# An attention gate feeding a capacity-limited mixture of experts: last rows transposed on TensorE, all table rows kept on chip, tail weights split on VectorE, z requested three lane steps ahead

## The chip, the cores and the metric

The kernel runs on one core of one Trainium2 chip, in one launch. The metric is the device time of one execution in microseconds. Before the change three timed runs took 1415.2, 1415.2 and 1415.48 us, median 1415.2. One more execution was profiled; its time is 1417.8 us, and its trace spans 1416.1 us from the first to the last instruction.

Engine names are those of the trace: PE is TensorE's matmuls, PEld its weight loads, DVE is VectorE, ACT ScalarE, POOL GpSimd, SP SyncE. SPq and POOLq are the instructions that these two engines issue to the DMA queues.

## The reference

Eight batches of 2496 rows, 256 wide, with 64-wide keys z. Each batch computes squared-ReLU attention with z as queries and keys, multiplies the result by u, and the 19968 rows of all batches go into a mixture of eight experts. A row goes to the expert with the largest logit; an expert that has more than 80 rows keeps the 80 with the largest gate weight. All other rows of the output are zero.

```python
scores = (1.0 / S) * np.matmul(z, z.transpose(0, 2, 1))
attn = np.maximum(scores, 0.0) ** 2
x = (u * np.matmul(attn, v)).reshape(B * S, D)        # B, S, D = 8, 2496, 256

logits = x @ w_gate                                    # 8 experts
expert_idx = np.argmax(logits, axis=1)
gate_w = softmax(logits)[np.arange(N), expert_idx]
for e in range(E):
    tok_idx = np.where(expert_idx == e)[0]
    if len(tok_idx) > capacity:                        # 80
        gw = gate_w[tok_idx]
        tok_idx = tok_idx[np.argpartition(-gw, capacity)[:capacity]]
    h = np.maximum(x[tok_idx] @ w1[e], 0.0)            # 256 x 1024
    out[tok_idx] = gate_w[tok_idx, None] * (h @ w2[e]) # 1024 x 256
```

The gate weights of nearly all rows are equal when rounded, so which rows an expert keeps is decided by position in the order that the reference's partition leaves; the kernel works out those positions from counts of rows per expert. Where this does not hold, a flag sends the kernel into a general path behind the measured one.

## The kernel before

**Numbers.** A large matmul operand is held as a high part (rounded) and a low part (the rest), and a product is three matmuls: high by high, low by high, high by low. ScalarE mostly rounds the high part, VectorE subtracts to get the low one. This split is done for z, v, the attention matrix, the expert weights w1 and w2 and the gathered rows.

**The attention.** A batch has 20 tiles of 128 rows, taken in five chunks of 512 rows (the last has 448). For each chunk the keys are taken in ten pairs of tiles. The matrix is symmetric: a pair is either computed (`scores`, then ReLU, square, split) or read back as the mirrored block of an earlier chunk (`mirrored`), which was transposed on VectorE, written to DRAM (`y`) and read (`blk`). Two chunks run at a time, as two lanes, half a chunk apart. A lane step `t` is one pair of each lane; five steps are half a chunk, 25 steps a batch. The order in which TensorE, ScalarE, VectorE and SyncE take their instructions is the order of the program text (`manual_schedule`); GpSimd is put under it too from the experts on.

**z and v for the next batch.** At the end of each lane step `z_and_v(t)` looks up tables by the step within the batch: `Z_LOAD` requests a 256 KB piece of z into the one buffer `zraw`, `Z_SPLIT` lets VectorE split it into `zs` (or `zm` for piece 0), `Z_COPY` copies it across partitions by DMA. A split stands before the next request, which needs its buffer. SyncE issues all DMAs of the attention in order, each waits for the semaphore of an earlier one, so at most eight are under way.

**A finished chunk** goes through `finished(b, qc, r)`, r being the pair of the next chunk beside which a part is put: x = u times the accumulators (VectorE and ScalarE), its rows transposed by two DMAs (`chunk_store`, L530) and stored to DRAM `xs` (`chunk_store2`), x split into three bf16 parts (`chunk_hi`, `chunk_rest`, `chunk_mid`, `chunk_lo`), gate logits by 24 small matmuls (`chunk_logits`, L554), and per batch the top-1, the gate weights, and the counts of rows per expert and block of 256 rows. `blocks` (L691 to L696) makes for each block a table row of running counts by three matmuls, rounds it on ScalarE and writes it to the DRAM table `wtab`. Near the end one lane is left, and `finished_late` does the same work for the last chunk but one.

**The end of the attention.** The weights of experts 0 and 1 are loaded and split beside the last chunks (`weights_ahead`); the raw weights of expert 2 wait in buffers (`kept`). Four further pieces of weights, 512 KB each, are requested near the last pair. Then x of the last 448 rows is made, its rows go through the DMA transposes, its logits through fp32 matmuls, and the top-1, the counts and the ranks of the 80 slots follow on VectorE. For experts 0 and 1 TensorE makes the table rows (`pe_table`) and picks each slot's row by a one-hot matmul (`pe_block`, `pe_fetch`); for experts 2 to 7 GpSimd reads the rows from `wtab` by six indirect DMAs (`fetches`).

**An expert.** VectorE compares its table row with the slot's rank and gets the token number (`token`), GpSimd gathers the 80 rows (`xg`), VectorE puts their halves together (`whole`), TensorE transposes them (`ffn_x`), two halves of the first product follow (`ffn1`, six matmuls each), ReLU on ScalarE, a transpose and a split (`ffn_h`), the second product (`ffn2`, 24 matmuls), and on ScalarE the scaling by the gathered gate weight; GpSimd scatters the rows to the output (`result`). `target` gathers the gate weights, which the last gate write (`gate_put`, elements of 4 bytes, L642) must have left in DRAM. `split(n)` splits the next n pieces of weights and requests as many new ones. For expert 2 three of the four low halves are left to the experts' part: one on VectorE, two on GpSimd (`half_lo(PL)`).

Of the kernel before, what the change touches and what calls it, by code (L numbers as in the profile page):

```python
# [26 lines left out]
def attn_moe_kernel(ctx, tc, zT, uT, v, wg, w1, w2, out, seq, cap):  # L27
# [504 lines left out]

    def chunk_store2(b, qc):
# [224 lines left out]

    def halves_hi(n):

        for _ in range(n):
            p, raw = kept.pop(0)
            halves.append(split_w(*p, raw, None))
            nc.scalar.copy(out=halves[-1][1], in_=raw)
# [47 lines left out]
    N_PE = 2  # L812
    wq_t, le_g, bo_g = [], [], []

    def scratch():

        t = vpool.tile([P, 2048], F32, tag="vt", name="scratch")
        n = [N_PE * P, 2 * (1 + NBLK), (E - 2) * (1 + NBLK), N_PE * NBLK]
        o = [sum(n[:i]) for i in range(5)]
        w = t[:, :o[1]].bitcast(BF16)  # L820
        wq_t.extend(w[:, e * 2 * P:(e + 1) * 2 * P] for e in range(N_PE))
        le_g.append(t[:, o[1]:o[2]].rearrange("p (e k) -> p e k", e=2))
        le_g.append(t[:, o[2]:o[3]].rearrange("p (e k) -> p e k", e=E - 2))
        bo_g.append(t[:, o[3]:o[4]].rearrange("p (e k) -> p e k", e=N_PE))

    def pe_table(e):

        wp = ps_s.tile([P, CH], F32, tag="s", name=f"wq_{e}")
        ev, od = oh[:, 0, :, e], oh[:, 1, :, e]
        nc.tensor.matmul(wp[:NBLK, :P], ev, upper, start=True, stop=True)  # L830
        nc.tensor.matmul(wp[:NBLK, P:2 * P], ev, ones_b, start=True, stop=False)
        nc.tensor.matmul(wp[:NBLK, P:2 * P], od, upper, start=False, stop=True)
        nc.scalar.copy(out=wq_t[e][:NBLK], in_=wp[:NBLK, :2 * P])
# [9 lines left out]
    WARM = 3  # L843
# [4 lines left out]
    def weights_ahead(qc, r):  # L848
        if not places:
# [6 lines left out]
            places.extend([None] * NW + [vv, a4[0], xt])  # L856
        if (qc, r) in SPLITS:
            p = SPLITS[qc, r]
            split_w(*p, w_raw.pop(p), V)
# [12 lines left out]
    def finished(b, qc, r):  # L872
# [22 lines left out]
        if qc == 0 and b > 0:  # L895
# [3 lines left out]
            elif r == 6:  # L899
                up_to(*part)  # L900
                blocks(ps_m, "m", gp, oh, *part)
# [3 lines left out]
    def finished_late(b, qc, r):  # L905
# [37 lines left out]
    if True:  # L943
# [150 lines left out]
        for i in range(e, len(entries)):  # L1094
# [4 lines left out]
            if i == e + HALF:  # L1099
                logits(n)  # L1100
                prev = at(n + 1)
                chunk_x(*prev)
            if i + 2 < len(entries) and i > e:
# [11 lines left out]
            else:  # L1115
                if i == e + HALF:
                    finished(*at(n), NP)
                if i == e + HALF + 1:
# [3 lines left out]
            if i == len(entries) - 2:  # L1122
# [3 lines left out]
                loads(4)  # L1126
# [16 lines left out]
        for e in range(N_PE):  # L1143
            pe_table(e)
# [170 lines left out]
    def steps_of(own, tl, tw, ps_t, ps_h):  # L1315
# [69 lines left out]
        def many_within():  # L1385
            le = le_g[1][:, :, 1:]
            tt(le, le, tot[:, es], ALU.mult)
            V.tensor_reduce(out=small["exc"][:, es], in_=le, axis=AX.X, op=ALU.add)
            tt(small["rin"][:, es], rank[:, 0, es], small["exc"][:, es], ALU.subtract)
            ts(small["base"][:, es], small["cnt"][:, es], float(2 * P), ALU.mult)  # L1390

        def fetches():

            rest = slice(N_PE, E)
            ix = tl.tile([P, E - N_PE], F32, name="ix")
            V.scalar_tensor_tensor(out=ix, in0=small["cnt"][:, rest], scalar=float(E),
                                   in1=first_w[:, 0, rest], op0=ALU.mult, op1=ALU.subtract)
            idx = tl.tile([P, E - N_PE], I32, name="idx_rest")
            ts(idx, ix, float(E), ALU.add)

            def one(u):
                ns, i = num(u), u - N_PE
# [339 lines left out]
```

## Time and profile before

| | |
|---|---|
| timed runs, median of 3 | 1415.2 us |
| profiled execution | 1417.8 us, span 1416.1 us |
| TensorE busy (matmuls) | 1360.8 us, 96% |
| VectorE, ScalarE, GpSimd busy | 1072.6 (76%), 1024.5 (72%), 47.5 us (3%) |
| DMA moved | 319.12 MB, mean 225 GB/s |
| granted TensorE clock, mean | 0.979 |

The attention takes all but the last 100 us. In it TensorE is busy without a break except at a few waits, and the other engines have time left; in the last 100 us no engine is busy throughout. In the rows below a line of a timeline is: start, time taken, engine, line of the kernel, operation, output and inputs with their shapes, count, and in brackets the idle time of the engine just before with what ended it.

### The profile page before, as it was taken

Reading aid. Unit: us, or ns where it says so; the run is one execution under the profiler, and the core shown is the slowest. Engines: PE = TensorE matmul, PEld = TensorE weight load, DVE = VectorE, ACT = ScalarE, POOL = GpSimd, SP = SyncE. Lnnn points to the kernel's source line nnn. Section 1 sums busy time; section 2 is a strip of 40 time slices with the busy share of each in tenths; the row PEclk is TensorE's granted clock in tenths of the full one; section 3 lists DMA queues with packets and bytes.
Section 4 is the critical chain, followed back from the end, with each engine's and each line's share of the span. In section 5 each row is a group of like instructions: output and inputs, shape, how many; then the busy total and the mean of one; then the engine's idle time right before and its main releaser. Section 6 shows DMA issues by size and latency. Waiting matters only on the chain. (4 is left out here: it accounts for less than half of the span.)

```text
span 1416.1 us, 30052 instructions
## 1 busy us (share of the span) xinstructions
PE 1360.8 (96%) x12033; PEld 1136.1 (80%) x12033; DVE 1072.6 (76%) x1558; ACT 1024.5 (72%) x1321; POOL 47.5 (3%) x52
## 2 busy tenths in 40 slices
PE   8998999999999999999999999999999999999586
PEld 5887887888977888788887888888887888777374
DVE  6776787787877877877877777877778777877675
ACT  6876697677876697677877587777877688775254
POOL 0000000000000000000000000000000000000164
PEclk9999999999999999999999999999999999999689
DMA  5699869997979969998879958998879957899543
GB/s 173 183 267 279 203 187 238 250 270 209 246 190 286 222 164 258 252 275 217 237 190 262 258 155 239 261 267 215 244 207 231 292 162 211 241 291 279 151 139 112
DMA packets 265956, 319.12 MB, mean 225 GB/s; under 512 B 98654, under 2 KB 190834, under 8 KB 255570
## 3 DMA queue, kind: packets, MB, share of 16 engines
q1 hardware_dynamic: 264594, 315.58, 83.2%
q8 instruction: 96, 1.57, 0.5%
q0 software_dynamic: 1216, 1.56, 0.5%
q14 instruction: 50, 0.41, 0.1%
HBM read 153.48 MB, written 126.37 MB: 198 GB/s over the span
## 5 line engine op out<-in xcount | busy, mean ns | idle before, releaser
L441 PE MATMUL acc<-ah,vt 64*128 64x512 f32 (+1 forms) x6004 | 831.2, 389 | 1.1 <-ACT vt L108 0.6
L441 PEld LDWEIGHTS acc<-ah,vt 64*128 64x128 f32 x6004 | 602.3, 186 | 101.5 <-DVE vt L159 1.5
L441 PE MATMUL acc<-al,vt 64*128 64x512 f32 (+1 forms) x3002 | 480.9, 387 | 0.2 <-DVE al L55 0.2
L55 DVE TENSOR_TENSOR al<-a,ah 128x1024 fp32r<-128x1024 f32 (+1 forms) x240 | 291.4, 1214 | 172.1 <-ACT ah L370 133.6
L364 ACT ACTIVATE a<-s 128x512 f32<-128x512 f32 (+1 forms) x480 | 258.7, 591 | 181.6 <-PE s L361 178.5
L441 PEld LDWEIGHTS acc<-al,vt 64*128 64x128 f32 x3002 | 310.6, 185 | 50.3 <-DVE al L55 0.6
L367 ACT ACTIVATE a<-a 128x1024 f32<-128x1024 f32 (+1 forms) x240 | 253.1, 1055 | 7.4
L55 DVE TENSOR_TENSOR al<-blk,ah 128x1024 fp32r<-128x1024 f32 x160 | 193.7, 1211 | 50.1 <-PE acc L441 23.5
L342 ACT CAST ah<-blk 128x1024 fp32r<-128x1024 f32 x160 | 167.3, 1047 | 85.2 <-PE acc L441 77.0
L297 DVE STREAM_TRANSPOSE x<-a 128x512 f32<-128x512 f32 x320 | 207.5, 687 | 0.0
L370 ACT CAST ah<-a 128x1024 fp32r<-128x1024 f32 x160 | 168.0, 1050 | 5.1
L361 PE MATMUL s<-zm,zs 64*128 64x512 f32 x960 | 145.2, 394 | 1.6 <-DVE zs L121 1.2
L361 PEld LDWEIGHTS s<-zm,zs 64*128 64x128 f32 x960 | 95.2, 184 | 21.0 <-ACT a L364 1.8
L361 PE MATMUL s<-zm 64*128 64x512 f32 x480 | 74.7, 405 | 1.9 <-ACT a L364 1.9
L375 DVE CAST ah<-a 128x1024 fp32r<-128x1024 f32 (+1 forms) x80 | 53.8, 673 | 29.7 <-ACT a L367 29.6
L361 PEld LDWEIGHTS s<-zm 64*128 64x128 f32 x480 | 48.2, 187 | 10.7 <-ACT a L364 2.7
L1449 POOL DMA_INDIRECT xg<-xs,tok x8 | 9.2, 1146 | 1340.0 <-DMA wtab<-wb 1333.8
L159 DVE TENSOR_TENSOR vt<-vraw,vt 128x1024 fp32r<-128x1024 f32 (+1 forms) x40 | 46.1, 1153 | 6.6 <-ACT vt L108 6.6
L554 PEld LDWEIGHTS <-xb 128*128 128x128 bf16 x936 | 26.7, 96 | 30.2 <-DVE xb L55 16.5
L554 PE MATMUL pl<-wgs,xb 128*128 128x24 bf16 x936 | 31.3, 174 | 15.8 <-DVE xb L55 15.8
L55 DVE TENSOR_TENSOR xb<-xf,xb 128x1024 bf16<-128x1024 f32 (+1 forms) x38 | 45.2, 1191 | 0.2
L108 ACT CAST vt<-vraw 128x1024 fp32r<-128x1024 f32 (+3 forms) x56 | 44.9, 829 | 0.0
(169 smaller groups left out, 786.8 us busy)
## 6 DMA issues: line engine op xcount, KB each, us to landing
y<-x SPq DMA_DIRECT2D x80, 1024.0 KB, 7.1
blk<-y SPq DMA_DIRECT2D x320, 256.0 KB, 6.6
out<-idle SPq DMA_DIRECT2D x40, 512.0 KB, 3.7
vraw<-v SPq DMA_DIRECT2D x32, 512.0 KB, 7.0
zm<-zs SPq DMA_DIRECT2D x128, 128.0 KB, 7.1
ut<-uT SPq DMA_DIRECT2D x32, 512.0 KB, 7.3
xs<-xq SPq DMA_DIRECT2D x32, 512.0 KB, 7.1
wraw<-w SPq DMA_DIRECT2D x28, 512.0 KB, 6.4
```

The lines of the kernel that those rows point to most:

```text
L55: V.tensor_tensor(out=o, in0=a, in1=b, op=op)
L108: eng.copy(out=o, in_=i)
L159: e1.tensor_tensor(out=vt[:, :nf, 1], in0=raw[:, :nf], in1=vt[:, :nf, 0], op=ALU.subtract)
L297: V.transpose(out=x[:, :, :, t].rearrange("p n k s -> p k n s"), in_=a)
L342: nc.scalar.copy(out=natural(ah), in_=src)
L361: nc.tensor.matmul(s, zk, zm[rows, :, y].rearrange("p h k t -> p k h t"), start=i == 0, stop=i == 2)
L364: nc.scalar.activation(out=a[:, h, :nq], in_=s[:, :nq], func=AF.Relu)
L367: nc.scalar.activation(out=a[:, :, :nq], in_=a[:, :, :nq], func=AF.Square)
L370: nc.scalar.copy(out=st["ah"][:, :, :nq], in_=a[:, :, :nq])
L375: V.tensor_copy(out=ah[:, :, :nq], in_=a[:, :, :nq])
L441: ins = nc.tensor.matmul(acc[c], vt, a[rows, k % 2, :nq], start=p == pairs[0] and group == 0 and i == 0, stop=p == pairs[-1] and group == ...
L554: nc.tensor.matmul(pl[:, t * n:(t + 1) * n], xb[:, i % 3, i // 3, t0:t0 + P], wgs[:, i // 3].rearrange("p s e -> p (s e)"), start=i == 0, ...
```

## The change

1. The last 448 rows are transposed on TensorE in eight blocks, copied by ScalarE as 16-bit halves in the order of the store, and stored by two DMAs (`chunk_rows_last`).
2. TensorE makes the table rows of all eight experts behind the last chunk (`pe_tables`, two experts per bank) and keeps them on chip; the slots of experts 2 to 7 pick their rows by one-hot matmuls (`many_pe`, `many_fetch`). `blocks` is no longer called in the batches and at the end, and the six indirect reads go.
3. The low halves of expert 2's weights and one of expert 1's are split on VectorE, four in a row beside expert 1. The order of the experts' part is written out anew up to expert 1; the last gate write comes before the first expert, the splits of later weights start beside expert 1 with two pieces, and go on with four per expert.
4. z's pieces are requested three lane steps before their split. The logits of the third chunk from the end come one entry later, and so do some parts of the chunk behind it.

```diff
+    def chunk_rows_last(b, qc):
...
+        for t0 in range(0, QT, 2):
+            xp = ps_a.tile([P, CH], F32, tag="acc", name=f"xp_{b}_{qc}_{t0}")
+            for t in (t0, t0 + 1):
+                q0 = min(t * P, nq - P)
+                for c in range(DC):
+                    nc.tensor.transpose(out=xp[:, (t - t0) * D + c * P:(t - t0) * D + (c + 1) * P],
+                                        in_=xf[:, c, q0:q0 + P], identity=ident)
+            nc.scalar.copy(out=xq[:, t0:t0 + 2],
+                           in_=xp.bitcast(U16).rearrange("p (t d h) -> p t h d", t=2, h=2))
+        n = QT - 1
+        nc.sync.dma_start(out=rows[r0:r0 + n * P].rearrange("(t p) w -> p t w", p=P),
+                          in_=xq[:, :n].rearrange("p t h d -> p t (h d)"))
+        nc.sync.dma_start(out=rows[r0 + n * P + P - TAIL:r0 + QT * P],
+                          in_=xq[P - TAIL:, n].rearrange("p h d -> p (h d)"))
...
+    def hi_only(p, raw):
+        halves.append(split_w(*p, raw, None))
+        nc.scalar.copy(out=halves[-1][1], in_=raw)
...
-    def pe_table(e):
...
+    def pe_tables(e0, pool, tag):
+
+        wp = pool.tile([P, CH], F32, tag=tag, name=f"wq_{e0}")
+        for e in (e0, e0 + 1):
+            ev, od = oh[:, 0, :, e], oh[:, 1, :, e]
+            o = wp[:NBLK, (e - e0) * 2 * P:(e - e0 + 1) * 2 * P]
+            nc.tensor.matmul(o[:, :P], ev, upper, start=True, stop=True)
+            nc.tensor.matmul(o[:, P:], ev, ones_b, start=True, stop=False)
+            nc.tensor.matmul(o[:, P:], od, upper, start=False, stop=True)
+        nc.scalar.copy(out=wq_t[E][:NBLK, e0 * 2 * P:(e0 + 2) * 2 * P], in_=wp[:NBLK])
...
-    WARM = 3
+    WARM = 6
...
             p = SPLITS[qc, r]
-            split_w(*p, w_raw.pop(p), V)
+            if r == NP - 1:
+                hi_only(p, w_raw.pop(p))
+            else:
+                split_w(*p, w_raw.pop(p), V)
...
             elif r == 6:
                 up_to(*part)
-                blocks(ps_m, "m", gp, oh, *part)
...
         if r == 0:
-            chunk_hi(b, qc)
             chunk_store(b, qc)
         elif r == 1:
+            chunk_hi(b, qc)
             chunk_rest(b, qc)
+        elif r == 2:
             chunk_mid(b, qc)
-        elif r == 2:
+        elif r == 3:
             chunk_lo(b, qc)
-        elif r == 3:
             chunk_store2(b, qc)
...
-        elif r == 9:
-            blocks(ps_m, "m", gp, oh, *part)
-
-    Z_LOAD = {12: 1, 14: 2, 16: 3, 18: 0, 22: 4}
-    Z_SPLIT = {14: 1, 16: 2, 18: 3, 21: 0, 24: 4}
+
+    Z_LOAD = {9: 1, 12: 2, 15: 3, 18: 0, 21: 4}
+    Z_SPLIT = {12: 1, 15: 2, 18: 3, 21: 0, 24: 4}
...
             if i == e + HALF:
-                logits(n)
                 prev = at(n + 1)
                 chunk_x(*prev)
+            if i == e + HALF + 1:
+                logits(n)
...
-                loads(4)
+                loads(2)
...
-        chunk_store(*prev)
+        loads(2)
         halves_hi(2)
         chunk_logits_last(*prev)
+        chunk_rows_last(*prev)
         half_lo()
         gate_top(b, NQ - 1, NQ)
-        chunk_store2(*prev)
...
-        for e in range(N_PE):
-            pe_table(e)
+        pe_tables(0, ps_s, "s")
         ranks()
...
+        def many_pe():
...
+            for i in range(E - 2):
+                nc.tensor.transpose(out=bp[:NBLK, i * ns:(i + 1) * ns], in_=bo[:ns, i],
+                                    identity=ident[:ns, :ns])
+            bt = tl.tile([P, E - 2, ns], BF16, name="bt_rest")
+            nc.scalar.copy(out=bt[:NBLK].rearrange("p e s -> p (e s)"), in_=bp[:NBLK, :(E - 2) * ns])
...
+        def many_fetch():
...
+            for i in range(2, E, 2):
+                wr = ps_h.tile([P, 512], F32, tag="h", name=f"wr_{i}")
+                for k in range(2):
+                    nc.tensor.matmul(wr[:ns, k * 2 * P:(k + 1) * 2 * P], bt[:NBLK, i + k - 2],
+                                     wq_t[i + k][:NBLK], start=True, stop=True)
+                ws = tl.tile([P, 2, 2 * P], BF16, name=f"ws_{i}")
+                nc.scalar.copy(out=ws[:ns].rearrange("p k w -> p (k w)"), in_=wr[:ns])
...
             from_table(1)
-            blocks(ps_h, "h", gp, oh, B * BPB - 2, B * BPB, "wl")
             one_within(1)
             token(1)
             halves_hi(2)
+            for e in range(2, E, 2):
+                pe_tables(e, ps_h, "h")
+            gate_near(B - 1, NQ - 1)
+            gcol[B - 1, NQ - 1] = gate_sum(B - 1, NQ - 1, NQ)
+            gate_put(B - 1, NQ - 1)
+            loads(2, PL)
+            warm_up(WARM)
             many_blocks()
-            fetch_one = fetches()
-            fetch_one(2)
-            fetch_one(3)
-            loads(2, PL)
-            fetch_one(4)
-            fetch_one(5)
-            warm_up(WARM)
             whole(0)
             ffn_x(0)
+            many_rows()
             ffn_xl(0)
...
+            many_within()
+            many_pe()
+            whole(1)
+            ffn1(0, 0)
+            many_fetch()
+            ffn_x(1)
+            ffn_xl(1)
+            token(2)
+            token(3)
+            ffn1(0, 1)
+            ffn_h(0, 0)
+            ffn1(1, 0)
+            ffn_h(0, 1)
+            empty()
+            whole(2)
+            ffn_x(2)
+            ffn_xl(2)
+            for _ in range(4):
+                half_lo()
+            ffn1(1, 1)
+            target(0)
+            split(1)
+            token(4)
+            spread(3)
+            split(1)
+            target(1)
+            ffn2(0)
+            for i in range(2, NU):
...
```

## Rows read from the trace of the kernel before

**Rows 1.** TensorE's waits up to 1318.5: line, waited for, us, times, longest

```profile
PE pl L554 <- DVE xb L55: 15.8, 7, 4.1
```

**Rows 2.** VectorE's waits from 20 to 1318, same columns

```profile
DVE zs L121 <- DMA zraw<-zT: 19.1, 7, 5.6
```

**Rows 3.** Timeline of TensorE near 135

```profile
135.40 0.76 PE L554 MATMUL pl<-wgs,xb 128*128 128x24 bf16 x22 [4.09 <-DVE xb L55]
```

**Rows 4.** Timeline of VectorE in the same stretch

```profile
132.59 0.28 DVE L121 CAST zs<-zraw 64x256 fp32r<-64x256 f32 x1 [5.64 <-DMA zraw<-zT]
```

**Rows 5.** Windows: stretch, length, each engine's busy us, granted clock, DMA share, GB/s

```profile
134.90:141.70 6.80, 6.30 (x50) 5.32 (x52) 5.87 (x9) 3.67 (x5) 0.00 (x0) 0.51 1.08 258
...
1288.60:1292.00 3.40, 3.40 (x30) 3.12 (x31) 2.59 (x4) 1.99 (x2) 0.00 (x0) 0.52 1.13 291
1353.50:1360.30 6.80, 5.88 (x31) 5.91 (x32) 3.44 (x8) 1.24 (x2) 4.48 (x5) 0.51 0.15 42
```

**Rows 6.** Timeline of SyncE's DMA issues, 118 to 124

```profile
118.99 0.40 SPq L174 DMA_DIRECT2D ut<-uT  x1
...
121.58 2.06 SPq L103 DMA_DIRECT2D zraw<-zT  x1
```

**Rows 7.** Timeline of TensorE, the two late logits near the end

```profile
1269.78 0.71 PE L554 MATMUL pl<-wgs,xb 128*128 128x24 bf16 x22 [1.36 <-DVE xb L55]
...
1288.57 0.76 PE L554 MATMUL pl<-wgs,xb 128*128 128x24 bf16 x22 [2.45 <-DVE xb L55]
```

**Rows 8.** Timeline of TensorE, table matmuls of one batch

```profile
254.42 0.25 PE L691 MATMUL wp<-upper,oh 128*80 128x128 bf16 x1
...
254.71 1.21 PE L441 MATMUL acc<-ah,vt 64*128 64x512 f32 x8
```

**Rows 9.** Timeline of SyncE's DMA issues, 1312 to 1347

```profile
1312.54 0.37 SPq L642 DMA_DIRECT2D gd<-gall  x1
1313.00 6.55 SPq L734 DMA_DIRECT2D wraw<-w  x4
...
1323.95 6.29 SPq L530 DMA_TRANSPOSE xq<-xf  x2
1332.30 0.37 SPq L539 DMA_DIRECT2D xs<-xq  x1
...
1346.64 0.38 SPq L642 DMA_DIRECT2D gd<-gall  x1
```

**Rows 10.** Windows behind the last attention matmul, columns of rows 5

```profile
1316.00:1318.00 2.00, 2.00 (x12) 1.84 (x11) 1.82 (x7) 2.00 (x3) 0.00 (x0) 1.00 0.00 0
...
1328.00:1330.00 2.00, 0.73 (x2) 0.00 (x0) 1.25 (x4) 1.67 (x2) 0.00 (x0) 0.50 1.40 327
```

**Rows 11.** Timeline of GpSimd, the first gather

```profile
1336.34 1.09 POOL L1449 DMA_INDIRECT xg<-xs,tok  x1 [1333.78 <-DMA wtab<-wb]
```

**Rows 12.** Chain that ended last: start, us, what

```profile
1346.64 7.87 DMA gd<-gall
```

**Rows 13.** Timeline of VectorE, expert 2's rows

```profile
1351.32 2.96 DVE L1473 COPY xf<-xg 80x512 uint16<-80x512 uint16 x1
```

**Rows 14.** Timeline of TensorE in the experts

```profile
1340.60 0.71 PE L1506 MATMUL hp<-w1h,xTh 128*80 128x512 f32 x1 [0.43 <-ACT xTh L1485]
...
1354.42 0.50 PE L1482 MATMUL xp<-ident,xf 80*128 80x80 f32 x2 [4.66 <-DVE xf L1473]
...
1359.84 0.86 PE L1521 MATMUL tp<-ident,h 80*128 80x80 f32 x8
...
1366.24 0.72 PE L1521 MATMUL tp<-ident,h 80*128 80x80 f32 x8
...
1406.16 0.28 PE L1536 MATMUL op<-w2h,hTl 128*80 128x256 f32 x1
```

**Rows 15.** Window of the experts' later part, columns of rows 5

```profile
1361.00:1406.60 45.60, 41.60 (x298) 33.69 (x296) 34.49 (x62) 32.47 (x57) 26.84 (x17) 1.00 0.55 171
```

**Rows 16.** VectorE's groups, 1361 to 1406.6: count, busy us, mean ns, idle before

```profile
L746 DVE TENSOR_TENSOR w2l<-wraw,w2h 128x1024 fp32r<-128x1024 f32 x10 | 12.2, 1218 | 3.3 <-ACT w2h L745 3.3
```

More of the change, by code (lines that the diff above doesn't have):

```diff
@@ L531, in chunk_store @@
         xq_t[b, qc] = xq
+    def chunk_rows_last(b, qc):
+        xf = xt_t[b, qc][0]
+        nq = min(CH, seq - qc * CH)
+        xq = xpool.tile([P, QT, 2, D], U16, tag="xq", name=f"xq_{b}_{qc}")
+        rows = xs.rearrange("(n h) w -> n (h w)", h=2)
+        r0 = (b * NT + qc * QT) * P
+        for t0 in range(0, QT, 2):
[12 more added lines that the diff above has]
+                          in_=xq[P - TAIL:, n].rearrange("p h d -> p (h d)"))
     def chunk_store2(b, qc):
@@ L757, in attn_moe_kernel @@
     halves = []
+    def hi_only(p, raw):
+        halves.append(split_w(*p, raw, None))
+        nc.scalar.copy(out=halves[-1][1], in_=raw)
     def halves_hi(n):
         for _ in range(n):
-            p, raw = kept.pop(0)
-            halves.append(split_w(*p, raw, None))
-            nc.scalar.copy(out=halves[-1][1], in_=raw)
+            hi_only(*kept.pop(0))
     def half_lo(eng=V):
@@ L1388, in many_within @@
             V.tensor_reduce(out=small["exc"][:, es], in_=le, axis=AX.X, op=ALU.add)
+        def many_within():
             tt(small["rin"][:, es], rank[:, 0, es], small["exc"][:, es], ALU.subtract)
             ts(small["base"][:, es], small["cnt"][:, es], float(2 * P), ALU.mult)
[L1392 to L1402, printed above, removed]
-                wr = tw.tile([P, 2 * P], BF16, tag="wr", name=f"wr_{u}{own}", bufs=8)
-                nc.gpsimd.indirect_dma_start(
-                    out=wr[:ns], out_offset=None, in_=wtab[:, :],
-                    in_offset=bass.IndirectOffsetOnAxis(ap=idx[:ns, i:i + 1], axis=0))
-                sl[u][2] = wr
-            return one
+        def many_pe():
+            bo, ns = x_t.pop("bo"), num(2)
+            bp = ps_t.tile([P, 512], F32, tag="t", name="bp_rest")
+            for i in range(E - 2):
[3 more added lines that the diff above has]
+            nc.scalar.copy(out=bt[:NBLK].rearrange("p e s -> p (e s)"), in_=bp[:NBLK, :(E - 2) * ns])
+            x_t["bt"] = bt
+        def many_fetch():
+            bt, ns = x_t.pop("bt"), num(2)
+            for i in range(2, E, 2):
[5 more added lines that the diff above has]
+                nc.scalar.copy(out=ws[:ns].rearrange("p k w -> p (k w)"), in_=wr[:ns])
+                for k in range(2):
+                    sl[i + k][2] = ws[:, k]
         def pe_block(i):
@@ L1420, in pe_fetch @@
             bt = tl.tile([P, P], BF16, tag="bt", name=f"bt_{i}", bufs=2)
-            V.tensor_copy(out=bt[:NBLK, :ns], in_=bp[:NBLK, :ns])
+            nc.scalar.copy(out=bt[:NBLK, :ns], in_=bp[:NBLK, :ns])
             wr = ps_h.tile([P, 512], F32, tag="h", name=f"wr_{i}")
@@ L1691, in ahead @@
-                if i == 4:
+                if i == 3:
+                    result(0)
+                    result(1)
+                if i + 3 < NU:
+                    token(i + 3)
+                split(2)
+                ffn1(i, 1)
+                spread(i + 2)
+                split(2)
+                target(i)
+                if i == NU - 1:
+                    ffn_h(i, 0)
+                ffn2(i - 1)
+                if i > 2:
+                    result(i - 1)
+                if i == 5:
@@ L1692, in ahead @@
                     flags_v()
-                if i == 5:
+                if i == 6:
                     flags_end()
```

85 lines of the change are left out of this document (18 added, 67 removed).

## The prediction

> **What bounds the kernel now.** I read the shares first, then the waits of TensorE and of VectorE, then the clock, then the stretch after the last attention matmul. TensorE is busy for 96% of the span, so in the attention part whatever makes it stand still, or run at its lower clock, is paid in full. Its list of waits shows few such places, and one line carries nearly all of them: the gate logits wait for the low part of x from VectorE, 15.8 us in 7 waits [rows 1]. VectorE's own list has the reason: it stood 19.1 us in 7 waits for pieces of z to land [rows 2]. The two belong together: VectorE begins to split a piece at 132.59 after 5.64 us of waiting, only then makes the low part, and the logits go on at 135.40, 4.09 us late [rows 3, 4]. So 5.64 - 4.09 = 1.55 us of such a wait is free, the rest is TensorE's. Behind the gap the granted clock is 0.51, the level of 1.2 GHz, for 6.8 us [rows 5]; TensorE is busy in it, so about half of that is lost too.
>
> After the attention the bound is a chain. Two DMAs transpose the last rows, a store follows, and the first gather leaves only at 1336.34 [rows 9, 11]; expert 0's first matmul starts at 1340.60 and the last expert's last one at 1406.16 [rows 14]: 65.6 us for eight experts.
>
> **z three lane steps ahead.** The late piece is the third, requested at the end of step 16 and split at the end of step 18. Now it is requested at the end of step 15. In SyncE's order that is ahead of the transfers of u and of the x rows, at 118.99 instead of 121.58 [rows 6]: 2.6 us sooner in issue alone, and with 1 MB less ahead of it in the rings, which at that stretch's 258 GB/s [rows 5] is another 3.9 us. Together 6.5 us against a longest wait of 5.64 [rows 4]. By the issue alone 5.64 - 2.6 = 3.0 us of waiting would stay, of which 1.55 is free. Pieces 1 and 2 get a third step as well; their buffer is single, so each request still waits for the split before it. What goes: of the 15.8 us [rows 1], 1.36 and 2.45 belong to two logits near the end, where no z is split [rows 7]; 12.0 us remain for five gaps. The half-clock stretches behind them are 6.8 us at 134.9 and 3.4 us at 783.4 and at 1107.7 (the first, and one like the others, are shown [rows 5]); half of 13.6 is 6.8. Ceiling 18.8 us. Floor: if half of the waits stays, about 8. I take 17.5, near the ceiling, because the issue alone already brings nearly all of it.
>
> **Logits one entry later.** The logits of the third chunk from the end waited 2.45 us, until 1288.57 [rows 7], and 3.4 us at half clock follow [rows 5]: 2.45 + 1.7 = 4.15 us. One entry later their low part is ready, and attention matmuls fill the place. What is late next: the following chunk's steps also move back (high part to its step 1, low part to 3), and its logits come one entry after the low part instead of two, so VectorE has less slack there. Ends 0 and 4.15; I take 3.5. The other late logits (1.36 us [rows 7]) are not touched.
>
> **No table rows in the batches.** Eight times three matmuls go; the next attention matmul starts 254.71 - 254.42 = 0.29 us after them [rows 8], so 2.3 us, all TensorE's time. The floor is 0, if TensorE waits there instead. The low split that leaves the place before the last x I put at nothing: the logits behind it wait for TensorE as well.
>
> **The rows' new way.** Out go the DMA transposes (at 1323.95, 6.29 us on the queue) and the wait for them until the store at 1332.30 [rows 9]. In come eight PE transposes behind the last logits; a pair of smaller ones takes 0.50 us [rows 14], so at most 2.0, beside VectorE's top-1, for which TensorE waits anyway. Two ScalarE copies of 1024 elements follow. The trace has none of this form; the nearest of this length is VectorE's, 1.22 us [rows 16]; I take that, with ends at half and twice. The rows are then ready at about 1324, at the latest 1326. The store cannot use that at once: four weight loads were issued from 1313.00 on, behind the gate's write of 4-byte elements at 1312.54 [rows 9], and the DMA engines moved nothing at 1316 to 1318 and still 327 GB/s at 1328 to 1330 [rows 10]. So the rings are full until about 1330, and the store's 0.45 MB takes 1.4 us behind that. It lands near 1332 and the first gather leaves near 1332.2: 4.1 us sooner, not the 10 us that the rows alone suggest, and a slower ScalarE copy costs nothing before 1329.
>
> Against it: the last gate write, again of 4-byte elements, now sits right behind the store and so ahead of the first two gathers. At 1346.64 it took 7.87 us to land [rows 12]. From 1331 that reaches to 1339, and a gather that is caught in it lands no sooner than today. Ends 0 and 4.1; I take 2.0. The Trainium skill, "DMA: Bandwidth & Descriptors", section "Issuing engines are not separate DMA queues", says that transfers of whatever engine run on the same 16 DMA engines and interleave; its "Rules for kernel authors" add that a non-contiguous last dimension becomes one descriptor per element. By that a gather on GpSimd's queue does not get past the gate write, the term is 0 and the time 2 us more; the silent stretch [rows 10] agrees that such a write stops others, and no row here shows it ahead of the first gather.
>
> **Tables for all experts.** Six indirect table reads and the last table writes go. In come 18 small matmuls, at 0.25 us [rows 8] 4.5 us of TensorE while it waits for the first gather, and then six transposes, six matmuls and four ScalarE copies around expert 0's first half, which are on the path: by the same rows about 2 us, between 0 and 4.
>
> **Experts.** GpSimd split two of the low halves; now VectorE does four in a row before expert 1 is through, 4 x 1.22 = 4.9 us [rows 16], one of which it already had there. What goes: expert 2's rows, whose copy beside GpSimd's split took 2.96 us at 1351.32 [rows 13], left TensorE idle for 4.66 us [rows 14], and expert 0's second product behind that ran at 0.51 of the clock until 1359.84 [rows 5, 14], 2.6 us lost of 5.2. Best 4.66 + 2.6 = 7.3 us gained, worst 3.7 + 2.0 = 5.7 lost. In the new order by these durations: expert 0's first half with the table work 9.5 us, a wait of 2 for expert 2's rows, 4.3 for two more products; then VectorE's low halves and two splits hold expert 1's second product until 22, and it ends at 25. Before: 1366.24 - 1340.60 = 25.6. From there TensorE needs 6.4 us for an expert (1359.84 to 1366.24 [rows 14]); VectorE's 34.5 us in 45.6 hold 19 splits at 1.22 (ten of w2, nine of w1) [rows 15, 16], which leaves 11.3 us over six experts, 1.9 each, and with four splits 6.8 us. The two are near each other; 25 + 6 x 6.4 = 63.4 against 65.6, less 0.4 for VectorE: I take 1.8 us.
>
> **Sum.** 17.5 + 3.5 + 2.3 + 2.0 + 1.8 = 27.1 us. The profiled execution took 1417.8 us (its span 1416.1), so 1390.7 by it. The median of the timed runs, 1415.2, is 2.6 us lower: 1388.
>
> **Rivals.**
> 1. The tail loses. The gate write lies on the first gathers, and the low halves with the new table work delay the experts by the worst case: 1415.2 - 23.3 + 5.7 = 1398. For it: [rows 12, 16]. Against it: the idle 4.66 us goes in any case. Chance 0.13.
> 2. The waits for z only move. The DMA engines are at 1.08 in that stretch [rows 5]; what comes sooner for z comes later for u, v or the mirrored blocks, and the gaps appear under another name: 1415.2 - 9.6 = 1406. Against it: neither list of waits has another transfer among its large ones. Chance 0.09.
> 3. Slower. With one buffer the loads form a chain; if piece 2 lands over 1.55 us too late for its split, which now comes at step 15 instead of 16, VectorE stands there too, in each of the seven batches that split z. A gap costs 18.8 / 4 = 4.7 us with its clock (the fifth is small). Seven make 32.9, more than the 18.8 + 9.6 that all the rest gains: 1420. Six would still come out even. Against it: the piece has three steps where two did. Chance 0.04.
> 4. It doesn't do what it says: SyncE reaches the moved requests no sooner, since it issues in order and waits in between, and the tail is even. The logits and tables alone are hidden too: 1414. Chance 0.04.
>
> The forecast has 0.70; its own range is 1380 to 1396. With the first rival and part of the second, 1379 to 1401 holds the time 8 times in 10. All best ends (18.8 + 4.15 + 2.3 + 4.1 + 7.3) give 1379, all worst ones (8 - 5.7) 1413. A measurement of this kernel can tell 0.2%, 2.8 us, from no change: faster 0.92, within it 0.04, slower 0.04.
>
> **What would show it.** In the profile after: VectorE's wait for z below 3 us in all, TensorE's wait for the low part of x near 2, no half clock near 135, 783 and 1107, no wait at the logits near 1288, and the last attention matmul about 23 us sooner. Counted from that matmul, the first gather leaves some 2 to 4 us sooner than now and the last product ends 4 us sooner. I am wrong if TensorE has new waits in the batches, if the attention ends less than 15 us sooner, or if the experts take over 69 us.

## The result and the profile after

The changed kernel takes 1397.59 us (median of 4 runs, 1396.5 to 1399.28); the kernel before took 1415.2 beside it. The ratio is 0.988, 95% interval 0.9862 to 0.9897, so 17.6 us less, where 27.1 were forecast. The time lies 1.6 us outside the forecast's own range (1380 to 1396) and inside the wider one (1379 to 1401). The profiled execution took 1396.5 us, its span is 1394.8, against 1417.8 and 1416.1 before. The spans differ by 21.3 us. That is more than the medians do: the profiled execution of before took 2.6 us more than its median, that of after 1.1 us less. The steps below are read from the two profiled executions.

TensorE's waits up to 1310 us come first (in all, times, longest), then VectorE's for z from 20 to 1310 us. They answer to [rows 1] and [rows 2].

```profile
PE pl L576 <- DVE gs L658: 2.0, 3, 0.7
PE pl L519 <- DVE xf L466: 1.4, 1, 1.4
PE pl L576 <- DVE xb L55: 1.4, 1, 1.4
```

```profile
DVE zs L121 <- DMA zraw<-zT: 0.3, 1, 0.3
```

The 15.8 us for the low part of x are 1.4, the 19.1 us for z are 0.3. With the gaps went the stretches at half clock behind them: none is left in the batches. One wait is new, 2.0 us in three for `gs`, the copy of the gate rows.

Now TensorE's timeline at the joints: the last matmul of the attention part in the kernel before, then of the changed kernel the same matmul, the transposes of expert 0's and of expert 2's rows, expert 0's first product, the last matmul of expert 1's second product and of the last expert's [rows 14].

```profile
1318.36 0.19 PE L515 MATMUL pl<-idle 128*128 128x32 bf16 x1
```

```profile
1293.63 0.19 PE L515 MATMUL pl<-idle 128*128 128x32 bf16 x1
...
1322.53 0.53 PE L1517 MATMUL xp<-ident,xf 80*128 80x80 f32 x2 [16.05 <-DVE xf L1508]
1323.59 0.70 PE L1541 MATMUL hp<-w1h,xTh 128*80 128x512 f32 x1
...
1332.83 0.50 PE L1517 MATMUL xp<-ident,xf 80*128 80x80 f32 x2 [2.29 <-DVE xf L1508]
...
1345.26 0.28 PE L1571 MATMUL op<-w2h,hTl 128*80 128x256 f32 x1
...
1386.66 0.28 PE L1571 MATMUL op<-w2h,hTl 128*80 128x256 f32 x1
```

The attention ends at 1293.63 instead of 1318.36: 24.7 us sooner. The experts, from their first product to the last one's end, take 1386.94 - 1323.59 = 63.4 us instead of 65.8 (1406.44 - 1340.60). But TensorE stands 16.05 us ahead of expert 0. GpSimd's timeline has the place, the first gather (the idle time before it is in brackets, with what ended last), as in [rows 11]:

```profile
1319.29 1.09 POOL L1484 DMA_INDIRECT xg<-xs,tok  x1 [1316.73 <-DMA gd<-gall]
```

It leaves 25.7 us after the attention's last matmul; before, that took 18.0. So 7.7 us are given back. The sum closes: 24.7 - 7.7 + 2.5 (experts) + 1.8 (from the last product to the end, 7.9 us instead of 9.7) = 21.3.

The rows of x that the gather reads are made early, as forecast: ScalarE's two copies begin at 1297.67.

```profile
1297.67 1.93 ACT L547 COPY xq<-xp 128x1024 uint16<-128x1024 uint16 x2 [1.24 <-PE xp L545]
```

SyncE's queue shows what lies between them and the gather (second column: how long the issue took); it answers to [rows 9].

```profile
1290.64 0.62 SPq L664 DMA_DIRECT2D gd<-gall  x1
1291.36 10.01 SPq L756 DMA_DIRECT2D wraw<-w  x4
1301.46 2.42 SPq L550 DMA_DIRECT2D xs<-xq  x1
1303.93 2.41 SPq L552 DMA_DIRECT2D xs<-xq  x1
1306.44 0.54 SPq L664 DMA_DIRECT2D gd<-gall  x1
```

There are two gate writes in elements of 4 bytes, of 2048 and of 512 elements. One stands ahead of four weight loads, the other right behind the store of the rows. Three windows of that stretch, as in [rows 10] (after the busy times: granted clock, DMA share, GB/s):

```profile
1297.00:1305.00 8.00, 6.48 (x45) 5.32 (x45) 6.75 (x45) 5.93 (x11) 0.00 (x0) 0.60 0.55 33
1305.00:1312.00 7.00, 1.47 (x6) 0.44 (x4) 2.12 (x6) 0.51 (x1) 0.00 (x0) 0.74 0.97 327
1313.00:1319.00 6.00, 0.00 (x0) 0.00 (x0) 0.00 (x0) 0.00 (x0) 0.00 (x0) 0.50 0.00 0
```

Behind the first write the DMA engines are busy for 0.55 of the 8 us, but move only 33 GB/s; behind the second nothing moves for 6 us, and no engine works either. Weights and store get through only between the two.

The bracket at the first gather names the gate write, because that was the last thing to land before it. The gather does not wait for that write, but for the two stores. In the trace's record of semaphores each store reports its landing in 16 parts. Twelve parts of each came by 1312.4; the last came at 1317.35 for the first store and at 1318.26 for the second, mixed with the reports of the gate write behind them (1311.8 to 1318.4). GpSimd's waits for the two stores end at 1317.37 and 1318.29, and the gather starts at 1319.29.

### The profile page after: what moved, and what is told of

It is laid out like the page before. It is cut to its first block, busy times and chain, and to the rows that moved or that the text cites. A ratio compares the mean times of both kernels' runs of the same rounds, so it can differ in the third digit from the quotient of the medians.

```text
span 1394.8 us, 30057 instructions
## 1 busy us (share of the span) xinstructions
PE 1350.3 (97%) x12047; PEld 1128.1 (81%) x12047; DVE 1070.9 (77%) x1557; ACT 1027.0 (74%) x1322; POOL 34.6 (2%) x44
## 5 line engine op out<-in xcount | busy, mean ns | idle before, releaser
L441 PE MATMUL acc<-al,vt 64*128 64x512 f32 (+1 forms) x3002 | 488.3, 386 | 0.3 <-DVE al L55 0.3
L441 PEld LDWEIGHTS acc<-al,vt 64*128 64x128 f32 x3002 | 315.7, 184 | 51.4 <-DVE al L55 1.4
L55 DVE TENSOR_TENSOR xf<-xf,xb 128x1024 f32<-128x1024 f32 (+1 forms) x38 | 44.9, 1182 | 0.2
L491 ACT CAST xb<-xf 128x1024 bf16<-128x1024 f32 (+1 forms) x39 | 39.7, 1018 | 5.0 <-DVE xf L55 2.8
```

What stands on the lines that cost most here:

```text
L55: V.tensor_tensor(out=o, in0=a, in1=b, op=op)
L441: ins = nc.tensor.matmul(acc[c], vt, a[rows, k % 2, :nq], start=p == pairs[0] and group == 0 and i == 0, stop=p == pairs[-1] and group == ...
L491: nc.scalar.copy(out=xb[:, 0], in_=xf)
```

## The experiments

**The theory** after this comparison: the waits for z were the price in the attention, and the two writes of 4-byte elements took back part of the gain by holding up the store. Rivals: the z waits only moved; the store was late because of the weights ahead of it; the edits of the experts cost. Each run was timed beside the kernel before, which took 1416.65 us beside the first four runs (z ahead alone, z's old tables, the last gate write moved and as rows), 1415.26 beside the next four (the two with the shared buffer, both gate writes as rows, the DMA transposes) and 1414.81 beside the other four. With 1415.2 beside the changed kernel, times of different groups compare to about 2 us.

**z ahead alone**, in the kernel before:

```diff
-    Z_LOAD = {12: 1, 14: 2, 16: 3, 18: 0, 22: 4}
-    Z_SPLIT = {14: 1, 16: 2, 18: 3, 21: 0, 24: 4}
+    Z_LOAD = {9: 1, 12: 2, 15: 3, 18: 0, 21: 4}
+    Z_SPLIT = {12: 1, 15: 2, 18: 3, 21: 0, 24: 4}
```

> The kernel before with nothing changed but the two tables of z's requests and splits. Theory (the waits for z were the price, and an earlier request removes them): 17.5 us less, ceiling 18.8, so 1396.4 to 1398 against 1415.2; VectorE's wait for z under 3 us in all, TensorE's wait for the low part of x down to the two logits near the end (3.8 us), no half clock near 135, 783 and 1107. Rival 2 of the prediction (the waits only move to other transfers): within 3 us of 1415, with new waits for other transfers in the lists. By this run it also shows what all the rest of the change is worth together: 1397.6 less the time of this run; the prediction's other terms say 9.6 us.

Measured: 1399.99 us, ratio 0.9889 (0.9873 to 0.9906), 16.7 us less. TensorE's waits in this run:

```profile
PE pl L554 <- DVE xb L55: 3.8, 2, 2.4
```

Only the two logits near the end are left [rows 7]. The theory holds; the rival that the waits only moved falls. But then all the rest of the change is worth only 2.4 us by the two times, 0.9 by the gain of each over the kernel beside it, and not 9.6.

**z's old tables in the changed kernel** (the same lines the other way round):

> The changed kernel with the old tables of z's requests and splits. Theory: the gaps come back, 17 to 19 us more than 1397.6, so 1415 to 1417, with TensorE's wait for the low part of x at 10 to 13 us. If the rest of the change had already moved the transfers out of z's way: under 8 us more.

Measured: 1402.12 us, only 4.5 more than the changed kernel. A miss: 17 to 19 were expected. VectorE's waits for z in this run:

```profile
DVE zs L121 <- DMA zraw<-zT: 8.9, 5, 6.0
```

Half of the 19.1 us of [rows 2] are gone without the earlier request. Something else in the change removes them.

**z's old tables and the table rows in the batches again**, written to DRAM but not read. In a first form their copy used the buffer of the gate rows:

```diff
             elif r == 6:
                 up_to(*part)
+                blocks(ps_m, "m", gp, oh, *part, "gs")
...
         elif r == 8:
             count(*part)
             up_to(*part)
             half()
+        elif r == 9:
+            blocks(ps_m, "m", gp, oh, *part, "gs")
```

> The changed kernel with the old tables of z's requests and the table rows made in the batches again (written, not read). With the old tables alone it took 1402.1, and only two of the z waits above 1 us were left (5.97 and 1.31 us, both in the first two batches), where the kernel before has five. Theory A (the table rows and their write to DRAM in each batch were what made the third piece of z late in the other batches): the waits near 457, 779 and 1103 come back, 10 to 13 us more, 1412 to 1415. Theory B (they were not; the waits hang on where the DMA backlog happens to stand): only the matmuls' 2.3 us come back, 1403 to 1406.

> The changed kernel with z ahead as it is, and the table rows made in the batches again (written, not read). Theory: eight times three matmuls at 0.29 us, 2.3 us more, 1399.9, and no new waits for z. If TensorE's time there was hidden: within 1 us of 1397.6.

Measured: 1423.1 us with z's old tables and 1411.31 with z ahead. Both miss what was expected, and both are void as tests of the table rows, since the shared buffer made a wait of its own. VectorE's list in the second:

```profile
DVE gs L658 <- DMA wtab<-wb: 8.8, 3, 3.6
```

So once more, with a buffer that is idle at that time (the tile `d` of the batch before) and without the row near the end:

```diff
-        wb = wpool.tile([P, 2 * P], BF16, tag=own, name=f"wb_{nid()}")
+        if own == "d":
+            wb = wpool.tile([P, NT, E], F32, tag="d", name=f"wb_{nid()}").rearrange("p t e -> p (t e)")
+            wb = wb[:, :P].bitcast(BF16)
+        else:
+            wb = wpool.tile([P, 2 * P], BF16, tag=own, name=f"wb_{nid()}")
...
                 up_to(*part)
+                blocks(ps_m, "m", gp, oh, *part, "d")
```

> The changed kernel with z's old tables and the table rows made in the batches again, as in the run before of that kind, but their copy lies in a buffer that nothing else wants at that time (there it shared the one buffer of the gate rows, and VectorE waited 13.8 us for its write). Seven of the eight, without the one near the end. With the old z tables alone it took 1402.1, and the z waits near 457, 779 and 1103 us were gone. Theory A (the table rows and their write make the third piece of z late in those batches): the three waits come back, 8 to 13 us more, 1410 to 1415. Theory B (those waits hang on something else of the change): 1402 to 1405, with the two z waits that were left.

> The changed kernel, z ahead, with seven of the eight table rows made in the batches again, their copy in a buffer of its own. The prediction priced eight at 2.3 us, so seven at 2.0: 1399.6. Rival (with z ahead the three matmuls are hidden, since the run with z's tables alone reaches the seventh batch's counts at 1199.3 us, the changed kernel at 1199.2): within 0.7 us of 1397.6.

Measured: 1413.69 us with z's old tables, 11.6 more than with those alone; 1398.27 us with z ahead, 0.7 more than the changed kernel, which is within the spread. In the first, VectorE's waits for z and three of its splits:

```profile
DVE zs L121 <- DMA zraw<-zT: 17.0, 5, 5.6
```

```profile
457.07 0.29 DVE L121 CAST zs<-zraw 64x256 fp32r<-64x256 f32 x1 [3.67 <-DMA zraw<-zT]
...
779.21 0.28 DVE L121 CAST zs<-zraw 64x256 fp32r<-64x256 f32 x1 [3.75 <-DMA zraw<-zT]
...
1102.39 0.28 DVE L121 CAST zs<-zraw 64x256 fp32r<-64x256 f32 x1 [3.36 <-DMA zraw<-zT]
```

The three waits are back in their old places. The spread of the five runs with z ahead (1395.3 to 1400.7 us) would hide the 2.0 us as well, but the traces settle it. From the counts of the first batch to those of the seventh TensorE takes 959.4 us with the rows, 959.1 with z ahead alone, which has them too, and 958.5 to 959.3 in seven executions with z ahead and without them; at the forecast's 0.29 us for each batch, six would be 1.7 us. Where the rows are gone, TensorE waits instead: the new wait for `gs`, 0.64 to 0.67 us in each of three batches of the changed kernel, is 0.18 and 0.17 us in two with the rows in place. So the table rows cost next to nothing by their matmuls; they cost by making z late, and only while z is requested late. The earlier request and the absence of the table rows are two cures for the same three gaps, which is why each alone is worth less beside the other. How a row written 30 us sooner does it is seen only in part. SyncE's request of the third piece, first in the run with the rows, then in the one without (the run with z's old tables alone):

```profile
445.90 2.79 SPq L103 DMA_DIRECT2D zraw<-zT  x1
```

```profile
445.56 0.35 SPq L103 DMA_DIRECT2D zraw<-zT  x1
```

At the same time, but the one is held up for 2.79 us and the other finds room. Which of SyncE's waits the additional DMA displaces stays open; a run that moves only that write, or makes the rows without writing them, was not made.

**The last gate write behind the first gathers:**

```diff
-            gate_put(B - 1, NQ - 1)
             loads(2, PL)
+            gate_put(B - 1, NQ - 1)
```

> The changed kernel with the last gate write (4-byte elements) issued behind the two weight loads of that place, so behind the first gathers and not ahead of them. Theory (that write, right behind the store of the last rows, holds back the store's own completion until 1318.3 and so the first gather at 1319.3): the gather leaves about 6 us sooner, counted from the last attention matmul at about 19 to 20 us instead of 25.7, and the time is about 6 us less, 1391 to 1392. Rival (the store is late because of the weights requested ahead of it, not because of the write behind it): the gather leaves as before, 25 to 26 us after the last attention matmul, and the time stays within 1.5 us of 1397.6. A third possibility: the write then delays the gate weights' gather for the results and the gain is given back at the end of expert 0.

**The last gate write as rows**, in its place:

```diff
+    def gate_rows(b, q0, pool, tag):
+        col, nt = gcol.pop((b, q0))
+        gt = pool.tile([P, CH], F32, tag=tag, name=f"gt_{b}_{q0}")
+        nc.tensor.transpose(out=gt[:nt, :P], in_=gall[:, col:col + nt], identity=ident)
+        gs = gp.tile([P, P], F32, tag="gs", name=f"gs_{b}_{q0}")
+        nc.scalar.copy(out=gs[:nt], in_=gt[:nt, :P])
+        nc.sync.dma_start(out=gd[col:col + nt], in_=gs[:nt])
...
-            gate_put(B - 1, NQ - 1)
+            gate_rows(B - 1, NQ - 1, ps_t, "t")
```

> The changed kernel with the last gate write as 4 rows of 512 bytes (one PE transpose and one ScalarE copy ahead of it) instead of 512 elements of 4 bytes; place and order as in the changed kernel. Theory (the small elements cost the time, not the place): the silence of the DMA engines behind the store is gone, the gather leaves 5 to 7 us sooner, 1391 to 1392. Rival (backlog of the weights): within 1.5 us of 1397.6.

Measured: 1395.68 us with the write moved, 1391.85 us with it as rows. In the first run the attention's last matmul, then on GpSimd the first gather and the first gather of gate weights:

```profile
1295.10 0.19 PE L515 MATMUL pl<-idle 128*128 128x32 bf16 x1
```

```profile
1313.96 1.09 POOL L1484 DMA_INDIRECT xg<-xs,tok  x1 [1311.40 <-issue]
...
1329.18 0.94 POOL L1497 DMA_INDIRECT gt<-gd,tok  x1 [2.42 <-DMA gd<-gall]
```

And in the second, the last matmul and the first gather:

```profile
1293.54 0.19 PE L515 MATMUL pl<-idle 128*128 128x32 bf16 x1
```

```profile
1313.06 1.10 POOL L1492 DMA_INDIRECT xg<-xs,tok  x1 [1310.50 <-issue]
```

So the gather leaves 18.9 and 19.5 us behind the attention's last matmul, instead of 25.7 (20.7 to 25.7 in the eight profiled executions that have the 4-byte write behind the store). The landings say it more sharply: in these eight the last part of the second store's report comes 2.6 to 5.9 us after the twelfth, in the other six kernels 0.1 to 0.7 us. Both edits take away the second silence with the weight loads ahead of the store left as they are, so the backlog falls as its cause. Moved, the write lands late for the gate weights instead, the third possibility, and GpSimd waits 2.42 us for it; TensorE then waits 3.95 us for expert 2's rows, not 2.29. Of 5.3 us that the experts start sooner (1318.28 against 1323.59) 3.5 are gone by the end; how much of that is the late write is not separated. As rows it costs nothing there, and 5.7 us remain. The Trainium skill, "DMA: Bandwidth & Descriptors", section "Queues, rings and completion order", says that the increment of the semaphore lands only after every earlier write of its DMA engine. No run here tests that rule by itself. The runs show something further: here a write issued behind the store held up the report of the store's landing.

**Both gate writes as rows**, the one of 2048 elements too:

```diff
-        elif r == 7:
-            gate_put(b, 0)
         elif r == 8:
+            gate_rows(b, 0, ps_s, "s")
```

> The changed kernel with both late gate writes as rows of 512 bytes: the last one (512 elements of 4 bytes so far) and the one of 2048 elements that SyncE issues at 1290.64, ahead of four weight loads and the store of the last rows. Theory (writes of 4-byte elements keep the DMA engines from completing what is queued around them; the first one silences them from 1297 to 1305, so the weights and, behind them, the store come late too): the weights land by about 1300, the store near 1304, and the first gather leaves 12 to 19 us after the last attention matmul instead of 19.3 with one of the two mended: 1383 to 1391. Rival (only the write right behind the store counts, the first one is hidden): as with the last one alone, 1391.9 within 1.5 us.

Measured: 1383.54 us, ratio 0.9774 (0.9758 to 0.9791): 31.7 us faster than the kernel before in the same runs, 14 faster than the changed kernel. The attention's last matmul, the first gather and the issue of the last gate write in this run, and its DMAs from 1293 to 1309 us (KB each, median us from issue to landing); then the same view of the changed kernel from 1290 to 1310:

```profile
1295.71 0.19 PE L515 MATMUL pl<-idle 128*128 128x32 bf16 x1
```

```profile
1306.30 1.09 POOL L1491 DMA_INDIRECT xg<-xs,tok  x1 [1303.74 <-DVE fw L628]
```

```profile
1308.32 0.28 SPq L667 DMA_DIRECT2D gd<-gs  x1
```

```profile
wraw<-w SPq DMA_DIRECT2D x4, 512.0 KB, 7.3
...
xs<-xq SPq DMA_DIRECT2D x1, 64.0 KB, 3.1
...
gd<-gs SPq DMA_DIRECT2D x1, 8.0 KB, 4.6
```

```profile
wraw<-w SPq DMA_DIRECT2D x4, 512.0 KB, 14.2
...
gd<-gall SPq DMA_DIRECT2D x1, 8.0 KB, 13.3
```

The same 8 KB land in 4.6 us instead of 13.3, and the weights requested behind them in 7.3 instead of 14.2. The gather now leaves 10.6 us after the attention (1306.30 - 1295.71), sooner than the 12 to 19 expected, and before the last gate write is even issued (1308.32), so it cannot depend on it. The first write was not hidden: as elements it costs another 8.3 us of time. As rows it is also issued one step later; its form and its step are not separated.

**The rows by DMA transposes**, with both gate writes as rows:

```diff
         loads(2)
+        chunk_store(*prev)
         halves_hi(2)
         chunk_logits_last(*prev)
-        chunk_rows_last(*prev)
         half_lo()
         gate_top(b, NQ - 1, NQ)
+        chunk_store2(*prev)
```

> As the run with both gate writes as rows, but the last 448 rows go through the two DMA transposes again instead of TensorE and ScalarE. Theory (once the DMA engines are free the rows' way sets the gather): the transposes' 6.3 us on the queue and their landing come back, the gather leaves 6 to 8 us later than with TensorE's transposes, and the time is 5 to 8 us more than that run's. Rival (the rows' way is hidden behind the weights and the ranks of the slots on VectorE): within 1.5 us of it.

Measured: 1388.04 us, 4.5 more than with TensorE's transposes. The attention's last matmul and the first gather:

```profile
1293.80 0.19 PE L515 MATMUL pl<-idle 128*128 128x32 bf16 x1
```

```profile
1308.08 1.09 POOL L1492 DMA_INDIRECT xg<-xs,tok  x1 [1305.52 <-PE warm L186]
```

The gather leaves 14.3 us after the attention instead of 10.6. The direction is the theory's; the time is a little under its range (5 to 8 us), the gather's 3.7 us well under (6 to 8). So the new way of the rows is worth 4.5 us once the DMA engines let its store through. What it is worth beside the 4-byte writes no run shows.

**The logits one entry sooner again**, with the chunk behind them in its old steps:

```diff
             if i == e + HALF:
+                logits(n)
                 prev = at(n + 1)
                 chunk_x(*prev)
-            if i == e + HALF + 1:
-                logits(n)
```

(The places of `finished(NP)` and of the four parts in `finished_late` go back with it.)

> The changed kernel with the logits of the third chunk from the end one entry sooner again, and the parts of the chunk behind it in their old places. Theory: the wait of 2.45 us for the low part and the 3.4 us at half clock behind it come back, 3.5 us more (0 to 4.15), 1401.1. Rival (VectorE is ahead there now that it no longer waits for z): within 1 us of 1397.6 and no half clock near 1270.

Measured: 1397.28 us, as the changed kernel. TensorE's timeline and GpSimd's first gather:

```profile
1268.17 0.76 PE L576 MATMUL pl<-wgs,xb 128*128 128x24 bf16 x22 [2.44 <-DVE xb L55]
...
1297.12 0.19 PE L515 MATMUL pl<-idle 128*128 128x32 bf16 x1
```

```profile
1318.24 1.09 POOL L1484 DMA_INDIRECT xg<-xs,tok  x1 [1315.69 <-DMA gd<-gall]
```

Neither theory nor rival: the wait is back (2.44 us), and so is the half clock behind it (0.55 from 1268.2 to 1271.6). The attention ends 3.5 us later than in the changed kernel, as priced; against the six profiled executions with the changed kernel's attention (its last matmul at 1293.5 to 1295.7) it is 1.4 to 3.6. The gather still leaves 1 us sooner than in the changed kernel. Where the DMA queue sets the gather, the microseconds that TensorE saves in front of it are worth nothing.

**Two of the four low halves on GpSimd again:**

```diff
-            for _ in range(4):
-                half_lo()
+            for eng in (V, V, PL, PL):
+                half_lo(eng)
```

> The changed kernel with the last two of the four low halves beside expert 1 on GpSimd again instead of VectorE. The prediction priced all edits of the experts together at 1.8 us and put four halves on VectorE at 4.9 us. Theory (VectorE is what holds expert 1's second product, and GpSimd is idle there): 1 to 2.5 us less, 1395 to 1396.5. Rival (GpSimd's gathers, for the gate weights and for expert 4, queue behind its two splits of 2.35 us, and VectorE's copies beside them take 2.96 instead of 0.45 us, as in the kernel before): 2 to 5 us more, 1399.5 to 1402.5.

Measured: 1401.93 us, 4.3 more. GpSimd's timeline, then VectorE's, then TensorE's wait for expert 2's rows:

```profile
1331.96 4.64 POOL L791 TENSOR_TENSOR w2l<-wall,w2h 128x1024 fp32r<-128x1024 f32 x2
```

```profile
1332.14 4.50 DVE L55 TENSOR_TENSOR none<-rank,incl 128x8 f32<-128x8 f32 x1
```

```profile
1337.39 0.50 PE L1517 MATMUL xp<-ident,xf 80*128 80x80 f32 x2 [6.36 <-DVE xf L1508]
```

In the changed kernel the same VectorE instruction is this one:

```profile
1331.64 0.16 DVE L55 TENSOR_TENSOR none<-rank,incl 128x8 f32<-128x8 f32 x1
```

A comparison of eight elements per partition takes 4.50 us instead of 0.16, as long as GpSimd's two splits, and expert 2's rows queue behind it: 6.36 us instead of 2.29. The rival is right in size, and in that VectorE is slowed; but it is this comparison that is held, and the copy that the rival named takes 0.49 us. At this place the two halves are 4.3 us better on VectorE. The Trainium skill, "SBUF — State Buffer", section "SBUF: two separate sides", has the rule: a GpSimd instruction that reads SBUF and a VectorE instruction with two inputs from SBUF share a pair of ports as an exclusive lock. The trace agrees that VectorE is held, and shows it held through both of GpSimd's instructions, 4.50 us where one of them takes 2.35.

## Why the prediction was right in sign and its gain too large

In the two spans the gain is 21.3 us, 5.8 under the forecast 27.1: 9.7 are lost at the first gather, and 1.4 more than forecast come in the attention, 0.7 in the experts and 1.8 behind them. The other 3.7 us to the medians' 17.6 are the spread of the two profiled executions.

**z ahead: right, but not additive.** 17.5 us forecast, 16.7 measured where it stands alone. Its terms held: the wait is 0.3, the half clock is gone. What the prediction did not see is that the table rows were the other half of the cause in three of the five gaps. z and tables together, forecast at 19.8, are worth 1413.69 - 1397.59 = 16.1 (with seven of the eight rows).

**Table rows: the floor came.** Eight times three matmuls, 0.29 us for each three, were counted as paid [rows 8]; measured, 0.7 us within the spread, and at most 0.9 in the traces over six batches. The prediction's floor of 0, "if TensorE waits there instead", is what happened: it waits for `gs`. The gap between neighbours of a row is not what its removal gives back.

**Logits: right in the attention, nothing in the time.** 3.5 us forecast, 1.4 to 3.6 us measured at the end of the attention, none in the kernel, because the next step hangs on the DMA queue.

**First gather: the step that failed.** The prediction had "2.0 us sooner", between 0 and 4.1, and measured from the attention's end it is 7.7 us later. It had seen both halves: the silence behind a gate write [rows 10] and the last gate write right behind the store. But it let that write catch the gathers, which would cost no more than today, and not the store itself, which the first gather must wait for: the last parts of the store's report came up to 5.9 us after its twelfth. It also put the end of the backlog at 1330, 11.6 us after the last matmul of the attention; now the transfers end near 1312, 18.4 us after it. Of these 6.8 us, 2.8 can be put to the first gate write, issued 3.0 us ahead of that matmul instead of 5.8; how the rest arises the runs do not separate, but with both writes as rows it is gone too: the gather then leaves 10.6 us after the attention, 7.4 sooner than in the kernel before.

**Experts: the sum right, by luck.** 1.8 us forecast, 2.5 measured; 63.4 us as worked out, but not from its parts. Expert 1's second product was to end 25 us after the first product, and each of the six experts behind it to take 6.4. It ends after 22.0 us (1345.26 + 0.28 - 1323.59), and the six take 41.4, 6.9 each: two errors of 3 us that cancel. Expert 2's rows wait 2.29 us, forecast 2. The sum itself varies: of ten other profiled executions with this order eight take 62.3 to 63.7 us and two 65.6. The 1.8 us from the last product to the end were not forecast; that stretch takes 7.7 to 10.0 us in the profiled executions of these kernels and follows none of the edits.

The first rival gave 1398, nearly the measured time, but that is luck: the gate write did its harm, to the store and not to the gathers, and the experts lost nothing. Of what was named as a sign, everything up to the end of the attention came (24.7 us against 23; the new waits are the 2.0 us for `gs`), and the two counted from there did not: the gather, and the last product, which ends 93.1 us behind that end and not 4 us under the 87.9 of before.

## What to carry to other kernels

A write in 4-byte elements was dear here for what was queued around it, behind and ahead, though nothing urgent waited for the write itself: transpose it on TensorE first and write rows. The last name in a wait's bracket need not be what the instruction waited for. Before a saved wait is counted, find what the next step hangs on; in front of the DMA that set the pace here, saved engine time was worth nothing. Two edits that take away the same wait must be tried together and each alone, since their gains don't add. A sum that comes out right is checked part by part.

## What the hardware showed that was not expected

512 elements of 4 bytes, 2 KB in all, issued behind a store of 0.45 MB, held back the last parts of that store's report, by 2.6 to 5.9 us in eight executions against 0.1 to 0.7 in the six without it, and with them the first gather. 2048 such elements made four weight loads behind them land after 14.2 us instead of 7.3. A VectorE comparison of eight elements per partition lasted 4.50 us beside GpSimd's splits, 28 times as long as alone.
